# Attention and two MoE layers on one core: other instruction prices for the planner of the first three blocks

## The chip, the cores and the metric

The kernel runs on one core of a Trainium2 chip. The metric is the device time of the whole program in microseconds (us). Before the change it is 1163.88 us, the median of three runs (1162.69 to 1164.0).

The names in this text: PE is TensorE (matmul), DVE is VectorE, ACT is ScalarE, POOL is GpSimd, SP is SyncE, which issues the DMA transfers. L561 is line 561 of the kernel before. In the changed kernel every line from L185 on has a number that is one higher: L561 is L562 there.

## The reference

Three stages, one after the other, all in float32:

```python
x = attention(q, k, v, mem_k, mem_v)       # 4 batches, 8 heads, 768 positions of 64; chunks of 32 queries,
                                           # each with 16 keys to the left, 8 to the right, and 8 memory keys
x = x.transpose(0, 2, 1, 3).reshape(3072, 512)
h = x @ w_in                               # 512 x 2048
g = np.maximum(h, 0.0) + alpha * np.minimum(h, 0.0)
x = g @ w_out                              # 2048 x 512
return ((x @ w_a) * (x @ w_b)) @ w_o2      # 512 x 1536 twice, 1536 x 512
```

The weight matrices arrive as 64-bit floating-point words, and the kernel itself turns them into float32.

## The kernel before

**The work.** The 3072 tokens are cut into 24 attention units of 128 tokens, and these into blocks: two blocks of 2 units (256 tokens) come first, and then blocks of 4 units (512 tokens). A block's first products (`gemm1`, x times w_in, 16 of 128 output columns each) and second products (`gemm2`, g times w_out) follow on the attention of its units. Each product in the first MoE layer is made of three fp16 passes, high times high, high times low and low times high (`gemm3`, L925, L926, L927), so each operand is split into a high half on ACT (L361) and a low half on DVE (L365). The second MoE layer (`w_a`, `w_b`, `w_o2`) comes in a second phase with a planner call of its own.

**A unit of attention.** PE turns keys and queries (L728, L717), makes the scores (L752), turns the probabilities (L804) and multiplies by the values (L818). ACT copies the turned queries (L724) and exponentiates (L778). DVE takes the largest score (L768) and inverts the sums (L786, L789); the normalization is either one operation on DVE (L794) or four on ACT (L800). The copies out of PSUM, `kT`, `pT` and `x`, go to DVE (L657) or to ACT (L659). Then DVE takes the sizes of x for its scale (L827, L889, L896, L903; L329 to L340 turn a size into a power of two).

**A product of the first layer.** ACT evicts it twice (L942 to `g`, L945 to `t`), DVE joins the two (L948), ACT writes the high half (L954) and DVE the low half (L957) of `ghl`. A second product is evicted by DVE's L991 or ACT.

**The weights.** `chunk()` brings in one of 8 chunks of w_in, and later one of 8 chunks of w_out: a transfer of 1024 KB from SP (L483), the absolute value on ACT (L546), then on DVE L552 (w_in) or L556 (w_out), L561, L568 and L575, which turn the two words of a number into one float32. For w_in one scale serves all 8 chunks (`scale_w1`, L510 to L516), so no chunk is split before the last is read; a chunk of w_out has a scale of its own (sizes by ACT's L583). Then L361 and L365 split. The float32 values of w_in chunks are put together in the tile `w1` (`w_94` in the rows below), where the halves go too, and raw words of its chunks 4 to 7 lie in the tile of w_out's halves (`w_95`).

**The order.** No order is written by hand. `Schedule` is a list planner: each operation has an engine (or two to choose from), a price in us, a rank and what it depends on. `emit()` takes again and again the operation that can start first by the plan's own clock; ties go by rank. The rows of all five engines come out of this. The prices come from the table `took`:

```python
def dve(n, rate=1.04, pointers=0):
    return took["dve"] + 0.06 * pointers + n * rate / 1000
def act(n, pointers=0):
    return took["act"] + 0.09 * pointers + n * took["rate"] / 1000
def either(n):
    return {"DVE": dve(n), "ACT": act(n)}
```

`either` (L664) prices the copies and lets the plan give each one to DVE or ACT. The other entries are single prices: `tiny`, `itself`, `part` and `largest` for small DVE operations, `exp` and `scaled` for ACT's L778 and L800, `scores` and `values` for PE. The table is filled at L184 (it holds for the chunks of w_in and w_out and their scales), again at L1062 for each block (`SHORT` for the first three blocks, as `EXACT` is 3, `FULL` for the others), and with `SHORT` for the second phase.

Of the kernel before, what the change touches and what calls it, by code (L numbers as in the profile page):

```python
# [169 lines left out]
def pe(n, passes=1):  # L170
# [5 lines left out]
SHORT = dict(  # L176
    dve=0.07, act=0.06, rate=0.833, tiny=0.07, itself=0.09, part=0.09, largest=0.1,
    exp=0.357, scaled=0.267, scores=1.16, values=2.02,
)
FULL = dict(  # L180
    dve=0.15, act=0.17, rate=0.85, tiny=0.15, itself=0.16, part=0.2, largest=0.2,
    exp=0.57, scaled=0.42, scores=0.9, values=1.15,
)
took = dict(SHORT)  # L184


def dve(n, rate=1.04, pointers=0):
# [16 lines left out]
def tile_attention_moe_moe2(  # L204
# [29 lines left out]
    EXACT = 3  # L234
# [643 lines left out]
    def x_block(jb, x32, xhl, c0, rank):  # L878

        u0, nu = blocks[jb]  # L880
        p0 = c0 // P
        am = col(4)
        am1 = col()
        s, inv, iy = (col() for t in ("sx", "ix", "iy"))
        for i in range(nu):
            attention(u0 + i, *units[u0 + i], x32, p0 + i, am, rank + 0.1 * i)

        def largest():
            nc.vector.tensor_reduce(out=am1, in_=am[:, p0 : p0 + nu], axis=AX.X, op=ALU.max)  # L889

        sd.op(
            "DVE", took["largest"], rank, largest, [(x32, ("am", p0 + i)) for i in range(nu)], [(f"amx{jb}", 0)]
        )

        after = [
            lambda: nc.vector.tensor_tensor(out=s, in0=s, in1=ral, op=ALU.mult),  # L896
        ]
        scale(
            lambda: am1, s, inv, [(f"amx{jb}", 0), ("alpha", 0)], [(f"sx{jb}", 0)], after=after
        )  # L900

        sd.op(
            "DVE", took["tiny"], rank, lambda: nc.vector.tensor_tensor(out=iy, in0=inv, in1=iy0, op=ALU.mult),  # L903
            [(f"sx{jb}", 0), ("s_w1", 0)], [(f"iy{jb}", 0)],
        )
        for part in range(p0, p0 + nu):
            c = slice(part * P, (part + 1) * P)
            src = [(x32, part), (f"sx{jb}", 0)]
            sd.op(
                "ACT", act(512, 1), rank, lambda c=c: split_hi(x32.tile[:, :, c], xhl.tile[:, 0, :, c], s),  # L910
                src, [(xhl, ("h", part))],
            )
            sd.op(
                "DVE", dve(512, pointers=1), rank,
                lambda c=c: split_lo(x32.tile[:, :, c], xhl.tile[:, 0, :, c], xhl.tile[:, 1, :, c], s),
                src + [(xhl, ("h", part))], [(xhl, part)],
            )
        return iy
# [56 lines left out]
    def gemm2(jb, m, ghl, c0, n, iy, rank):  # L975
        ps, y32 = Buf(mm_slots), Buf(g_slots)
        c = slice(m * P, (m + 1) * P)
        d = slice(c0, c0 + n)
        iym = col()
        KQ = KF1 // 4  # L980

        def product(i):
            gh, gl = ghl.tile[:, 0, :, d], ghl.tile[:, 1, :, d]
            gemm3(
                ps.tile[:, :n],
                [(w2h[:, j, c], w2l[:, j, c], gh[:, j, :], gl[:, j, :]) for j in range(i * KQ, (i + 1) * KQ)],
                first=i == 0, last=i == 3,
            )

        def evac():  # L990
            nc.vector.tensor_scalar(y32.tile[:, :n], ps.tile[:, :n], iym, None, op0=ALU.mult)  # L991

        def evac_scale():
            nc.vector.tensor_tensor(out=iym, in0=iy, in1=inv_w2[:, m : m + 1], op=ALU.mult)

        t0 = blocks[jb][0] * P

        def store():
            nc.sync.dma_start(out=yd[:, m, t0 : t0 + n], in_=y32.tile[:, :n])

        for i in range(4):
            sd.op(
                "PE", KQ * pe(n, 3), rank, lambda i=i: product(i),
                [(ghl, (j, c0)) for j in range(i * KQ, (i + 1) * KQ)]
                + [(f"w2{2 * m}", 0), (f"w2{2 * m + 1}", 0)]
                + [("g1", jb, j) for j in range(KF1)], [(ps, 0)],
            )
        sd.op(
            "DVE", 0.07, rank - 1000, evac_scale,
            [(f"iy{jb}", 0)] + [(f"inv_w2{2 * m + i}", 0) for i in range(2)], [("iym", jb, m)],  # L1010
        )
        sd.op("DVE", dve(n, pointers=1), rank - 1000, evac, [(ps, 0), ("iym", jb, m)], [(y32, 0)])
        sd.op("SP", dma(n * 4 * P), -500, store, [(y32, 0)], [("yd", jb, m)])
# [32 lines left out]
    scaled = [chunk("w1", c, w_in, KD, CW, -5 + 0.5 * c, load_ranks[c]) for c in range(NC1)]  # L1046
# [12 lines left out]
            ar = 9 if b == 2 else (b - 1) * 10 + 4  # L1059
            place.append((Buf(x32_slots), Buf(xhl_slots), Buf(ghl_slots), 0, ar, b * 10 + 5, b * 10 + 8))  # L1060
    for jb, (x32, xhl, ghl, c0, ar, r1, r2) in enumerate(place):
        took.update(SHORT if jb < EXACT else FULL)  # L1062
        n = blocks[jb][1] * P
        iy = x_block(jb, x32, xhl, c0, ar)
        for m in range(KF1):
            gemm1(jb, m, xhl, ghl, c0, n, r1)
        for m in range(KD):
            gemm2(jb, m, ghl, c0, n, iy, r2)
# [334 lines left out]
```

## Time and profile before

| | us |
|---|---|
| runs | 1163.88, 1164.0, 1162.69 (median 1163.88) |
| the profiled execution | 1163.05 |
| its span, first to last instruction | 1161.3 |
| PE busy in it | 1116.2 (96%) |
| DVE busy | 874.9 (75%) |
| ACT busy | 595.5 (51%) |
| POOL busy | 232.3 (20%) |
| mean granted clock of TensorE | 0.982 |

Shares are averages over stages with different limits, so a stage is read by its own window. An instruction's duration can overlap the start of the next one on the same engine; the distance between two starts is what it costs in a full queue. An idle time in a row comes with what released the engine.

### The profile page before, as it was taken

The page shows a single profiled execution, that of the slowest core. Times are in us where ns is not written, and L with a number is a line of the kernel's source. Part 1 is how long each engine was busy: PE and PEld are TensorE (multiplying, and loading weights), DVE is VectorE, ACT ScalarE, POOL GpSimd, SP SyncE. Part 2 cuts the span into 40 slices and gives each one's busy share as a digit, 9 for nine tenths or more (in the row PEclk, how much of TensorE's full clock was granted, in tenths as well). Part 3 has the DMA queues.
Part 4 walks back from the last instruction along what each step waited for, and adds up shares of the span by engine and source line. Part 5 has one row for each costly group of instructions (what it writes and reads, how often), then busy time and mean ns, then how long its engine had stood idle before and what let it go on. Part 6 is the DMA issues. An engine that isn't in the chain of part 4 may idle for free.

```text
span 1161.3 us, 23129 instructions
## 1 busy us (share of the span) xinstructions
PE 1116.2 (96%) x9304; PEld 808.8 (70%) x9304; DVE 874.9 (75%) x1524; ACT 595.5 (51%) x1300; POOL 232.3 (20%) x298
## 2 busy tenths in 40 slices
PE   4499899999999999999999999999999999999998
PEld 3378786555555555544444688888888888888887
DVE  6999998887887888796352287876867958958882
ACT  4599767866786776486262122533424433424340
POOL 1000002022002111222300010243323424324530
PEclk8599999999999999999999999999999999999999
DMA  9964571548446823433603162613513514415211
GB/s 254 254 132 120 154 202 46 141 122 230 132 126 179 227 82 94 166 109 121 242 1 136 59 196 84 198 38 101 191 55 114 177 37 146 146 37 178 96 37 38
DMA packets 162523, 150.93 MB, mean 130 GB/s; under 512 B 104032, under 2 KB 139888, under 8 KB 162416
## 3 DMA queue, kind: packets, MB, share of 16 engines
q1 hardware_dynamic: 162416, 149.45, 42.9%
q8 instruction: 73, 1.20, 0.4%
q14 instruction: 34, 0.28, 0.1%
HBM read 120.33 MB, written 29.10 MB: 129 GB/s over the span
## 4 chain that ended last, share of the span: by engine, by line
PE 87%; DVE 7%; ACT 3%; DMA 1%; issue 1%; POOL 0%; SPq 0%; ACTq 0%; DVEq 0%; POOLq 0%
PE mm L925 27%; PE mm L927 27%; PE mm L926 26%; PE pair L804 2%; PE mm L818 2%; PE pair L728 1%; PE pair L752 1%; DVE w L568 1%; DMA w1b<-wb_d 1%; PE mm L717 1%; DVE w L365 1%; ACT sm L778 1%; DVE w L575 0%; DMA kw<-in_k_dram 0%; PE mm L324 0%
## 5 line engine op out<-in xcount | busy, mean ns | idle before, releaser
L927 PE MATMUL mm<-ghl,w 128*128 128x512 f16 (+1 forms) x448 | 156.2, 349 | 2.5 <-DVE w L365 2.5
L925 PE MATMUL mm<-xhl,w 128*128 128x512 f16 (+1 forms) x448 | 156.7, 350 | 1.3 <-ACT t L945 1.2
L926 PE MATMUL mm<-xhl,w 128*128 128x512 f16 (+1 forms) x448 | 156.6, 349 | 1.0 <-DVE xhl L365 1.0
L925 PE MATMUL mm<-ghl,w 128*128 128x512 f16 (+1 forms) x448 | 156.3, 349 | 0.3 <-ACT w L361 0.3
L927 PE MATMUL mm<-xhl,w 128*128 128x512 f16 (+1 forms) x448 | 156.5, 349 | 0.0
L926 PE MATMUL mm<-ghl,w 128*128 128x512 f16 (+1 forms) x448 | 156.2, 349 | 0.0
L927 PE MATMUL mm<-units,w1b 128*128 128x256 f16 x560 | 152.6, 273 | 0.7 <-DVE w1b L365 0.7
L926 PE MATMUL mm<-units,w1b 128*128 128x256 f16 x560 | 152.6, 273 | 0.0
L925 PE MATMUL mm<-units,w1b 128*128 128x256 f16 x560 | 152.6, 273 | 0.0
L927 PEld LDWEIGHTS <-w 128*128 128x128 f16 x896 | 87.8, 98 | 83.1 <-DVE w L365 3.4
L925 PEld LDWEIGHTS <-w 128*128 128x128 f16 x896 | 87.9, 98 | 75.0 <-ACT w L361 0.5
L926 PEld LDWEIGHTS <-w 128*128 128x128 f16 x896 | 87.8, 98 | 73.5 <-issue 1.6
L925 PE MATMUL mm<-w2b,w1b 128*128 128x256 f16 x504 | 137.4, 273 | 0.3 <-DMA w1b<-wb_d 0.2
L926 PE MATMUL mm<-w2b,w1b 128*128 128x256 f16 x504 | 137.4, 273 | 0.0
L927 PE MATMUL mm<-w2b,w1b 128*128 128x256 f16 x504 | 137.4, 273 | 0.0
L927 PEld LDWEIGHTS <-w1b 128*128 128x128 f16 x1064 | 104.1, 98 | 13.1 <-DVE w1b L365 0.9
L925 PEld LDWEIGHTS <-w1b 128*128 128x128 f16 x1064 | 104.1, 98 | 12.9 <-DMA w1b<-wb_d 0.8
L926 PEld LDWEIGHTS <-w1b 128*128 128x128 f16 x1064 | 104.1, 98 | 12.4
L381 POOL TENSOR_TENSOR raw<-w 128x256 f32<-128x256 f32 x18 | 15.3, 852 | 456.7 <-ACT raw L583 456.7
L957 DVE TENSOR_TENSOR ghl<-g,ghl 128x512 f16<-128x512 f32 (+1 forms) x112 | 69.3, 630 | 23.4 <-ACT ghl L954 23.1
L942 ACT ACTIVATE g<-mm 128x512 f32<-128x512 f32 (+1 forms) x112 | 60.5, 540 | 46.0 <-PE mm L927 43.8
L948 DVE SCALAR_TENSOR_TENSOR g<-t,columns,g 128x512 f32<-128x512 f32 (+1 forms) x112 | 77.1, 696 | 8.4 <-ACT t L945 8.2
(288 smaller groups left out, 2405.7 us busy)
## 6 DMA issues: line engine op xcount, KB each, us to landing
w1b<-wa_d SPq DMA_DIRECT2D x26, 896.0 KB
w1b<-wb_d SPq DMA_DIRECT2D x26, 896.0 KB
raw<-in_moe_w_out_dram SPq DMA_DIRECT2D x8, 1024.0 KB
kw<-in_k_dram SPq DMA_DIRECT2D x40, 176.0 KB
vw<-in_v_dram SPq DMA_DIRECT2D x40, 176.0 KB
qt<-in_q_dram SPq DMA_DIRECT2D x24, 256.0 KB
raw<-in_moe_w_a_dram SPq DMA_DIRECT2D x12, 512.0 KB
raw<-in_moe_w_b_dram SPq DMA_DIRECT2D x12, 512.0 KB
```

The source lines that it names most:

```text
L365: nc.vector.scalar_tensor_tensor(out=lo, in0=src, scalar=s, in1=hi, op0=ALU.mult, op1=ALU.subtract)
L381: (nc.vector if e == "DVE" else nc.gpsimd).tensor_tensor(out=out_()[:, i], in0=x()[:, a], in1=y()[:, b], op=op)
L568: nc.vector.scalar_tensor_tensor(out=f, in0=lo, scalar=29, in1=f, op0=ALU.logical_shift_right, op1=ALU.bitwise_or)
L717: nc.tensor.transpose(out=pq.tile[:, g * P : (g + 1) * P], in_=qt.tile[:, 2 * g : 2 * g + 2, :].rearrange("p h d -> p (h d)"), identity=ident,
L804: nc.tensor.transpose(out=heads(pp, P)[:KW, o, g], in_=sm.tile[:, o, g], identity=ident)
L818: nc.tensor.matmul(out=out[64 * o : 64 * o + 64, g, c], lhsT=vw.tile[:, j, 2 * g + o], rhs=pT.tile[:, o, g, c], start=True, stop=True,)
L925: nc.tensor.matmul(out=ps, lhsT=lh, rhs=rh, start=first and i == 0, stop=False)
L926: nc.tensor.matmul(out=ps, lhsT=lh, rhs=rl, start=False, stop=False)
L927: nc.tensor.matmul(out=ps, lhsT=ll, rhs=rh, start=False, stop=last and i == n - 1)
L942: nc.scalar.activation(out=g.tile[:, :n], in_=ps.tile[:, :n], func=ACTF.Relu, scale=E1)
L948: nc.vector.scalar_tensor_tensor(out=g.tile[:, :n], in0=t2.tile[:, :n], scalar=nal[:, m : m + 1], in1=g.tile[:, :n], op0=ALU.mult, op1=ALU ...
L957: nc.vector.tensor_tensor(out=ghl.tile[:, 1, m, d], in0=g.tile[:, :n], in1=ghl.tile[:, 0, m, d], op=ALU.subtract,)
```

## The change

A new table `REAL` is added. It takes the place of `SHORT` in two places: where `took` is first filled, and for the first three blocks.

```diff
 SHORT = dict(
     dve=0.07, act=0.06, rate=0.833, tiny=0.07, itself=0.09, part=0.09, largest=0.1,
     exp=0.357, scaled=0.267, scores=1.16, values=2.02,
 )
...
-took = dict(SHORT)
+REAL = dict(dve=0.09, act=0.14, rate=0.87, tiny=0.17, itself=0.18, part=0.2, largest=0.2, exp=0.32, scaled=0.30, scores=0.9, values=1.15)
+took = dict(REAL)
...
-        took.update(SHORT if jb < EXACT else FULL)
+        took.update(REAL if jb < EXACT else FULL)
```

No operation of the program is changed. The second phase's order is the same in both kernels, row for row, and so is the end of the first phase on every engine: the last 9707 of PE's rows, 646 of DVE's and 258 of ACT's are equal. The start is equal up to the second unit of attention. What moves lies between.

**ACT, where the first chunks of w_in are split.** L724 copies a unit's turned queries; `w_94<-raw` is the hi split of w_in's chunk 0, the three `w_94<-ghl` are those of chunks 1 to 3, and `w_522<-raw` is the absolute value of w_out's chunk 0. Before:

```order
L778 ACTIVATE sm,sums<-pair,nm 128x96 x8
L724 ACTIVATE qT<-mm 128x512
L361 ACTIVATE w_94<-raw,columns 128x4x256
L361 ACTIVATE w_94<-ghl,columns 128x4x256 x3
L942 ACTIVATE g<-mm 128x256
L945 ACTIVATE t_579<-mm 128x256
```

Now:

```order
L779 ACTIVATE sm,sums<-pair,nm 128x96 x8
L725 ACTIVATE qT<-mm 128x512
L547 ACTIVATE w_522<-raw 128x1024
L362 ACTIVATE w_94<-raw,columns 128x4x256
L362 ACTIVATE w_94<-ghl,columns 128x4x256 x3
L943 ACTIVATE g<-mm 128x256
L946 ACTIVATE t_590<-mm 128x256
```

The absolute value of a chunk of w_out has moved ahead of the four hi splits; before, it stands 25 rows below the first of them. The first copy of `pT` is in the same place.

**DVE, in the same place of the program.** L365 (now L366) is the lo split, L794 (L795) a normalization, L575 (L576) the last step of a chunk of w_in, here chunk 6, and L948 (L949) the join of a first product. Before:

```order
L516 TENSOR_SCALAR columns<-columns 128x1
L789 RECIPROCAL rs<-rs 128x8
L561 TENSOR_SCALAR w_94<-w_94 128x8x128
L903 TENSOR_TENSOR columns<-columns 128x1
L794 TENSOR_TENSOR sm<-sm,rs 128x384
L365 SCALAR_TENSOR_TENSOR w_94<-raw,columns,w_94 128x4x256
L365 SCALAR_TENSOR_TENSOR w_94<-ghl,columns,w_94 128x4x256 x2
L948 SCALAR_TENSOR_TENSOR g<-t_579,columns,g 128x256
L365 SCALAR_TENSOR_TENSOR w_94<-ghl,columns,w_94 128x4x256
```

Now:

```order
L795 TENSOR_TENSOR sm<-sm,rs 128x384 x2
L576 SCALAR_TENSOR_TENSOR w_95<-w_95,w_94 128x1024
L366 SCALAR_TENSOR_TENSOR w_94<-raw,columns,w_94 128x4x256
L366 SCALAR_TENSOR_TENSOR w_94<-ghl,columns,w_94 128x4x256 x3
L949 SCALAR_TENSOR_TENSOR g<-t_590,columns,g 128x256
L949 SCALAR_TENSOR_TENSOR g<-t_610,columns,g 128x256
L658 COPY kT<-pair 128x384
L958 TENSOR_TENSOR ghl<-g,ghl 128x256 x2
L658 COPY kT<-pair 128x384
L949 SCALAR_TENSOR_TENSOR g<-t_660,columns,g 128x256
L562 TENSOR_SCALAR w_94<-w_94 128x8x128
```

Both normalizations of the unit are here on DVE, L576 has come in between them and the lo splits (before, L575 of chunk 6 stands 11 rows above the first lo split, ahead of the scale's L329), all four lo splits come ahead of the first join, and an L562 of chunk 7 stands behind it.

**A copy of x that changes engines.** Some thirty rows later, while w_out's first chunk is read. On ACT before:

```order
L361 ACTIVATE w_94<-w_95,columns 128x4x256
L954 CAST ghl<-g 128x256
L942 ACTIVATE g<-mm 128x256
L945 ACTIVATE t_919<-mm 128x256
L546 ACTIVATE w_921<-raw 128x1024
L659 COPY x_261<-mm 128x4x128
L659 COPY kT<-pair 128x384
L954 CAST ghl<-g 128x256
```

On DVE now:

```order
L557 TENSOR_SCALAR w_522<-w_522 128x1024
L958 TENSOR_TENSOR ghl<-g,ghl 128x256 x2
L562 TENSOR_SCALAR w_522<-w_522 128x1024
L949 SCALAR_TENSOR_TENSOR g<-t_978,columns,g 128x256
L658 COPY x_261<-mm 128x4x128
L366 SCALAR_TENSOR_TENSOR w_94<-w_95,columns,w_94 128x4x256
L958 TENSOR_TENSOR ghl<-g,ghl 128x256
L828 TENSOR_REDUCE columns<-x_261 128x1
```

The copy of x was ACT's L659 and is now DVE's L658, ahead of its L828. Before, DVE's row ahead of that L827 is an L561.

## Rows read from the trace of the kernel before

**Rows 1.** The page: busy time of each engine.

```profile
PE 1116.2 (96%) x9304; PEld 808.8 (70%) x9304; DVE 874.9 (75%) x1524; ACT 595.5 (51%) x1300; POOL 232.3 (20%) x298
```

**Rows 2.** Busy time by window: us, PE, PEld, DVE, ACT, POOL, PEclk, DMA share, GB/s.

```profile
0.00:58.80 58.80, 26.51 (x239) 20.36 (x240) 45.07 (x84) 29.91 (x80) 4.99 (x41) 0.67 0.94 253
58.80:178.80 120.00, 112.87 (x1283) 97.30 (x1281) 112.51 (x241) 97.47 (x275) 0.00 (x0) 0.99 0.60 147
178.80:730.00 551.20, 551.20 (x3902) 311.20 (x3900) 395.00 (x671) 315.18 (x718) 82.27 (x96) 1.00 0.43 133
```

**Rows 3.** Timeline of PE: start, us, instruction, idle before it and its releaser.

```profile
168.33 0.28 PE L927 MATMUL mm<-ghl,w 128*128 128x256 f16 x1 [0.34 <-DVE w L365]
...
178.77 0.38 PE L925 MATMUL mm<-xhl,w 128*128 128x512 f16 x1
```

**Rows 4.** Timeline of DVE from 166 to 170.

```profile
166.40 0.68 DVE L657 COPY x<-mm 128x512 f32<-128x512 f32 x1
167.00 1.27 DVE L365 SCALAR_TENSOR_TENSOR w<-w,columns,w 128x1024 f16<-128x1024 f32 x1
168.19 0.68 DVE L827 TENSOR_REDUCE columns<-x 128x1 f32<-128x512 f32 x1
168.79 0.48 DVE L991 TENSOR_SCALAR g<-mm,columns 128x256 f32<-128x256 f32 x1
...
169.24 0.95 DVE L758 TENSOR_TENSOR sm<-pair,mask 128x768 f32<-128x768 f32 x1
```

**Rows 5.** Timeline of DVE from 53 to 59.

```profile
53.07 1.22 DVE L575 SCALAR_TENSOR_TENSOR w<-w,w 128x1024 int32<-128x1024 int32 x1
54.21 0.28 DVE L329 TENSOR_REDUCE m<-mm 128x1 f32<-128x128 f32 x1
54.52 0.15 DVE L333 TENSOR_SCALAR m<-m 128x1 int32<-128x1 int32 x1
54.71 0.15 DVE L337 TENSOR_SCALAR columns<-m 128x1 f32<-128x1 f32 x1
...
55.96 0.55 DVE L794 TENSOR_TENSOR sm<-sm,rs 128x384 f32<-128x384 f32 x1
57.25 1.28 DVE L365 SCALAR_TENSOR_TENSOR w<-raw,columns,w 128x1024 f16<-128x1024 f32 x1 [0.74 <-ACT w L361]
```

**Rows 6.** Timeline of ACT: first hi split of w_in, first L546 of w_out.

```profile
56.01 1.21 ACT L361 ACTIVATE w<-raw,columns 128x1024 f16<-128x1024 f32 x1 [3.04 <-DVE w L561]
...
74.11 1.23 ACT L546 ACTIVATE w<-raw 128x1024 f32<-128x1024 f32 x1
```

**Rows 7.** SyncE's issue of w_out's first chunks, and what DMA moved by window.

```profile
48.69 3.24 SPq L483 DMA_DIRECT2D raw<-in_moe_w_out_dram  x2
...
48.70:53.40 4.70, 1.32 (x9) 0.90 (x5) 4.54 (x10) 3.18 (x17) 0.00 (x0) 0.50 0.92 224
48.70:57.00 8.30, 1.94 (x11) 1.26 (x8) 7.51 (x20) 4.17 (x18) 0.00 (x0) 0.50 1.04 254
```

**Rows 8.** Timeline of DVE: two copies of kT.

```profile
63.52 1.01 DVE L657 COPY kT<-pair 128x384 f32<-128x384 f32 x2
```

**Rows 9.** Timeline of ACT: two evictions of 256 columns.

```profile
61.23 0.38 ACT L942 ACTIVATE g<-mm 128x256 f32<-128x256 f32 x1 [0.65 <-PE mm L927]
61.51 0.38 ACT L945 ACTIVATE t<-mm 128x256 f32<-128x256 f32 x1
```

**Rows 10.** Waits of DVE, 58.5 to 168.3: us in total, times, longest.

```profile
DVE w L556 <- ACT w L546: 1.4, 3, 0.7
DVE rs L786 <- ACT sm L778: 1.2, 1, 1.2
DVE g L948 <- ACT t L945: 1.0, 1, 1.0
DVE m L329 <- PE mm L324: 0.9, 2, 0.7
DVE w L568 <- ACT w L361: 0.8, 1, 0.8
```

## The prediction

> **What bounds the kernel now.** I read the totals first, then the stages, then the waits. TensorE (PE) is busy 96% of the span [rows 1], so everything that is not PE work is worth at most the rest. The windows show where that rest lies [rows 2]: 32 us before 58.8, in which weights are loaded and converted and the clock is 0.67; 7.1 us between 58.8 and 178.8; nothing at all from 178.8 to 730, where 551.20 of 551.20 us are busy. The reader should see two things in this. Between 58.8 and 178.8 VectorE (DVE) is as full as PE: 112.51 of 120 us (94%) beside 112.87, while ScalarE (ACT) has 97.47 (81%). And once 178.8 is passed, a delay of PE can't be won back, since PE has no idle time to give for 551 us.
>
> What happens at 178.8 is that block 2, the first of 512 tokens, starts its first product [rows 3]. In PE's order it stands behind all second products of the two small blocks, and those need all eight chunks of w_out. The last one to come is chunk 7: its low part is written by DVE from 167.00 to 168.3 [rows 4], PE's L927 starts at 168.33 after a wait for it, and block 2 starts 10.4 us later [rows 3]. So the time at which DVE is through with chunk 7 is what I forecast, and I take the shift of block 2 as the shift of the end. The instructions behind it stand in the same order in both kernels.
>
> **The change part by part.** The table changes only prices in the planner; the instructions do the same work. What counts is the order that comes out, and who does the copies that either DVE or ACT may do.
>
> *The start.* Before, ACT runs the first hi split (L361) at 56.01 and DVE the first lo split (L365) at 57.25 [rows 5, 6]. Now ACT has `w_522<-raw`, the absolute value of w_out's chunk 0, ahead of its four splits; before, that stood at 74.11 [rows 6]. And DVE has an L576 of 1024 elements ahead of its first L366, and L576 waits for the first hi split: both use the tile `w_94`, one reads and the other writes it. So four things of some 1.15 us come in series: the absolute value, a hi split, L576, then the lo split. The first can't begin before chunk 0 has landed. SyncE issues chunks 0 and 1 at 48.69 [rows 7]; the landing is in no row, so I bound it. From 48.7 to 53.4 the queues move 4.7 x 224 = 1053 KB, about one chunk: if all of it were chunk 0, it would land at 53.4. From 48.7 to 57.0 they move 8.3 x 254 = 2108 KB, two chunks: if both go side by side, chunk 0 lands at 57.0. Part of the early bytes belong to transfers issued before, so I take 55.6, a little over the middle. Then the absolute value ends at 56.75, the hi split at 57.9 and L576 at 59.1 (1.15, 1.15 and 1.2 from start to start; such rows take 1.21 to 1.28, of which some 0.08 overlap the next [rows 5, 6]), and the lo split starts at 59.1 in place of 57.25: **+1.8**. With 57.0 it would be +3.2. With 53.4 the scale that the split needs is the later one. Its chain starts at 54.21 behind an L575 of 1.14 [rows 5], and without L575 ahead of it and with L903 to L794 still to come, I estimate the end of the two L795 at 55.7; L576 follows to 56.85, and the lo split comes 0.4 earlier than now. So -0.4 to +3.2.
>
> One page weighs in here. The Trainium skill (DMA: Bandwidth & Descriptors, "Anatomy of one DMA") gives, for another way of issuing, about 2.0 us plus the bytes at 436 GB/s, which for a chunk of 1.05 MB is an estimated 4.4 us, a landing at 53.1 and so the -0.4. The rows disagree as to the rate: with a DMA share of 1.04 the queues move 254 GB/s from 48.7 to 57.0 [rows 7], and chunk 0 isn't alone in them. By the page the sum below would end 2.2 us lower, at +2.9 in place of +5.1.
>
> *The work ahead of chunk 7.* I count DVE's instructions from the first lo split of w_in to the lo split of chunk 7 in both orders. They are 216 now and 229 in the changed order. More: 3 copies of x (2 to 5), 3 of kT (4 to 7), one each of L561, L827, L758, L991, L889, L896 and L903, and one chain L329 to L340. Fewer: 3 normalizations L794 (8 to 5) and one L556. Prices are distances from start to start, or durations less the overlap of some 0.08. A copy of x is 0.60 (166.40 to 167.00), L827 0.60, L991 0.40 and L758 0.87 [rows 4]. Two kT copies take 1.01 together, 0.46 each [rows 8]. L561 and L556 are both one-input operations on 1024 elements and cancel. L794 is 0.47, an L329 0.31, and a small one such as L333 0.19 [rows 5]; there are six of these (L333, L337, L340, L889, L896, L903), 1.14. That makes 1.80 + 1.38 + 0.60 + 0.40 + 0.87 + 0.31 + 1.14 = 6.5 more, and 3 x 0.47 = 1.4 less: **+5.1**.
>
> Why copies go to DVE can be read off the table. A copy of 512 cost 0.60 on DVE and 0.49 on ACT in the plan; now it costs 0.62 and 0.585. A 256-wide eviction on ACT is planned at 0.363, while the two traced ones start 0.28 apart [rows 9] (0.273 in the old table). So 64 of them make ACT look 5.3 us busier than it is, and the planner relieves it at the cost of the engine that is fuller.
>
> *Waits.* DVE's waits in the stretch are listed [rows 10]. L948's 1.0 and L568's 0.8 come right behind the first splits. There the changed order has one more lo split ahead of its first L949, and L569 stands far behind its release, so I drop both: **-1.8**. The others (L556 1.4, L786 1.2, L329 0.9) may stay or go, and new ones may come; I keep them, with 0 and -3.5 as the far end. PE isn't what DVE would wait for: in the changed order PE has all 32 first products early and only two units' value products between them.
>
> *The sum.* +1.8 + 5.1 - 1.8 = +5.1: chunk 7's lo split ends at 173.4, block 2 starts at about 183.9. On the profiled execution, 1163.05 (its span of 1161.3 and 1.75 around it), this makes 1168.15. That execution lies 0.8 below the median of the runs shown; on the median's scale I forecast **1169.0**.
>
> **The rivals.** *(A) The plan is better, and DVE's waits go.* If intervals nearer to the traced ones place instructions where their data is ready, L556, L786 and L329 lose their 3.5 us. For it: all three are waits of DVE for ACT or PE that the old prices didn't foresee. Against it: the new prices of ACT are further from the rows than the old. It gives 5.1 - 3.5 = +1.6, or 1165.5; with a landing at 53.4 it is -0.6, or 1163.3. No difference.
>
> *(B) PE becomes the bound, and it is faster.* If DVE is through with chunk 7 early enough, PE loses its idle 7.1 us between 58.8 and 178.8 [rows 2], less the 1.5 or so by which the first product comes later. That is -5.6, or 1158.3 on the median's scale. It decides from the point at which chunk 7's lo split ends by 162.8 (178.8 - 5.6 - 10.4). For it: PE's order has fewer attention steps between the first products, so what waits for DVE comes later in it. Against it: DVE's own work, with none of the listed waits, still ends at 168.3 + 5.1 + 1.8 - 1.8 - 3.5 = 169.9. A weaker form, half of the gain, would need an early landing and two thirds of DVE's waits gone.
>
> *(C) The loss is larger.* DVE now has L562 of w_in's chunk 7 behind the fourth product, and copies of kT among the first products; everything on DVE queues behind such a wait. With the late landing (+1.4 over my value) and 2 us of new waits it is +8.5, or 1172.4.
>
> *(D) The change doesn't do what it says.* Its ACT prices aren't the traced intervals, as shown above. That is part of my forecast rather than another time.
>
> **How the numbers follow.** A difference under 0.2%, 2.3 us, can't be told from none here. My forecast, from +2.4 to +7, has 0.46; (C) 0.15; (A) 0.24; (B) 0.15, weak form included. That gives slower 0.61, same 0.24, faster 0.15. The range leaves out most of (B) and the far end of (C): from 1162.0, which takes in (A) with an early landing, to 1173.0. The forecast alone has 1166.3 to 1171.
>
> **What would show it.** In the changed kernel's trace: `w_522` on ACT beginning about 55.6 with a wait for a transfer, ahead of the first hi split; the first lo split of w_in near 59.1; 5 x copies on DVE and some 107 us of its work before the lo split of w_out's chunk 7, which ends near 173; PE's first 128x512 product near 183.8 and no idle time from there to 735. It is wrong if block 2 starts before 178.8, if DVE is idle for more than 6 us ahead of chunk 7, or if the end moves by another amount than block 2's start.

## The result, and the profile after

The changed kernel takes 1178.36 us (median of 4 runs, 1176.21 to 1179.74) beside 1163.85 for the kernel before: a ratio of 1.0125 with a 95% interval of 1.0113 to 1.0138. It is slower by 14.5 us. The prediction had 5.1 us, with an upper end at 1173.0: the sign was right, the size was a third of it. The profiled execution took 1178.0, 14.95 above that of before. One execution of n3 below (1681.72 us at a mean granted clock of 0.657) was in a slow state and is left out of n3's numbers; all other numbers are of fast runs.

Busy times on the page of the changed kernel, which answer to [rows 1]:

```profile
PE 1122.6 (95%) x9304; PEld 811.4 (69%) x9304; DVE 875.6 (74%) x1529; ACT 596.4 (51%) x1301; POOL 231.6 (20%) x298
```

PE does the same 9304 matmuls and is busy for 6.4 us longer. That isn't work: 5.4 of it lie between the first product and block 2, where the mean granted clock is 0.95 in place of 0.99, as the windows below show.

The timeline of the start, ACT and then DVE, against [rows 6] and [rows 5]:

```profile
55.09 1.14 ACT L547 ACTIVATE w<-raw 128x1024 f32<-128x1024 f32 x1 [2.75 <-DMA raw<-in_moe_w_out_dram]
56.14 1.21 ACT L362 ACTIVATE w<-raw,columns 128x1024 f16<-128x1024 f32 x1
```

```profile
57.38 1.23 DVE L576 SCALAR_TENSOR_TENSOR w<-w,w 128x1024 int32<-128x1024 int32 x1 [2.02 <-ACT w L362]
58.64 1.28 DVE L366 SCALAR_TENSOR_TENSOR w<-raw,columns,w 128x1024 f16<-128x1024 f32 x1
...
179.15 1.28 DVE L366 SCALAR_TENSOR_TENSOR w<-w,columns,w 128x1024 f16<-128x1024 f32 x1
```

The series of four is there: w_out's chunk 0 lands at 55.09, the hi split and L576 follow, and the first lo split starts at 58.64 in place of 57.25, 1.4 us later. The last row is w_out's chunk 7, whose lo split starts at 179.15 in place of 167.00 [rows 4].

The timeline of PE at its largest waits and at block 2's start, against [rows 3]:

```profile
59.98 0.40 PE L928 MATMUL mm<-xhl,w 128*128 128x256 f16 x1 [1.32 <-DVE w L366]
...
97.05 0.27 PE L926 MATMUL mm<-xhl,w 128*128 128x256 f16 x1 [2.05 <-ACT xhl L362]
98.44 0.34 PE L927 MATMUL mm<-xhl,w 128*128 128x256 f16 x1 [1.11 <-DVE xhl L366]
...
180.49 0.40 PE L928 MATMUL mm<-ghl,w 128*128 128x256 f16 x1 [2.30 <-DVE w L366]
...
192.38 0.38 PE L926 MATMUL mm<-xhl,w 128*128 128x512 f16 x1
```

Block 2 starts at 192.38 and not at 178.77: +13.6 of the 14.9 that the span grew by are there when it starts.

Windows of each kernel: from PE's first product to block 2's, from the first lo split to the end of chunk 7's, and from block 2's start to the point behind which PE's rows are the same in both kernels (columns as in [rows 2]). Before:

```profile
58.79:178.77 119.98, 112.85 (x1282) 97.29 (x1280) 112.49 (x241) 97.48 (x275) 0.00 (x0) 0.99 0.60 147
57.25:168.19 110.94, 103.95 (x1196) 89.54 (x1194) 103.58 (x216) 91.97 (x254) 0.00 (x0) 0.98 0.62 153
178.77:590.67 411.90, 411.90 (x2930) 216.15 (x2928) 321.67 (x549) 277.17 (x648) 76.70 (x88) 1.00 0.47 142
```

After:

```profile
58.03:192.38 134.35, 118.28 (x1279) 99.66 (x1277) 119.35 (x248) 100.50 (x279) 0.36 (x1) 0.95 0.54 132
58.64:180.34 121.70, 105.78 (x1181) 89.46 (x1180) 108.52 (x229) 94.33 (x259) 0.00 (x0) 0.96 0.57 140
192.38:605.67 413.29, 412.60 (x2931) 216.08 (x2929) 316.71 (x543) 274.41 (x641) 75.43 (x88) 1.00 0.47 141
192.38:1176.20 983.82, 977.50 (x7788) 691.09 (x7785) 713.87 (x1201) 465.31 (x939) 226.23 (x257) 1.00 0.38 120
```

These rows split the loss in two ways. By PE: between its first product and block 2's its idle time grows from 7.1 to 16.1 us (+8.9), its busy time from 112.85 to 118.28 (+5.4), and it starts 0.8 earlier; that is the 13.6. By DVE: its work up to chunk 7 grows from 103.58 to 108.52 (+4.9), its idle time from 7.4 to 13.2 (+5.8), and it starts 1.4 later; that is 12.1, and the rest of the 13.6 is half clock behind it. Both are accounts of where the time stands, and don't say what would come back if one term were taken away; the experiments ask that. The remaining 1.3 us come between block 2's start and 605.67 (413.29 us in place of 411.90).

The waits of DVE in that stretch, against [rows 10]:

```profile
DVE g L992 <- PE mm L928: 2.7, 4, 1.3
DVE m L330 <- PE mm L325: 2.0, 4, 1.2
DVE g L949 <- ACT t L946: 1.6, 2, 1.5
DVE x L658 <- PE mm L819: 1.3, 3, 0.6
DVE w L366 <- ACT w L362: 1.1, 2, 0.6
DVE kT L658 <- PE pair L729: 1.0, 2, 0.7
DVE pT L658 <- PE pair L805: 1.0, 2, 0.5
DVE w L569 <- PE mm L928: 0.6, 1, 0.6
DVE ghl L958 <- ACT ghl L955: 0.6, 1, 0.6
```

Before, the one wait for PE beside those of [rows 10] was this:

```profile
DVE pT L657 <- PE pair L804: 0.7, 2, 0.4
```

Before, DVE waited for ACT above all, and 1.6 us for PE. Now 8.6 of these 11.9 us are for PE, and 6.6 of the 8.6 come after 121, behind the last first product.

The clock, in a window of the kernel before and then in windows of the changed kernel (PEclk is the third number from the right):

```profile
60.00:62.00 2.00, 2.00 (x17) 1.62 (x16) 1.01 (x2) 1.35 (x4) 0.00 (x0) 0.83 0.94 232
```

```profile
62.00:64.00 2.00, 2.00 (x11) 1.40 (x10) 1.96 (x3) 1.20 (x4) 0.00 (x0) 0.50 0.81 211
64.00:66.00 2.00, 2.00 (x19) 1.73 (x17) 0.59 (x2) 1.28 (x4) 0.00 (x0) 0.91 1.18 314
...
96.00:98.00 2.00, 0.27 (x1) 0.10 (x1) 2.00 (x6) 1.49 (x4) 0.00 (x0) 1.00 0.99 249
98.00:100.00 2.00, 1.56 (x8) 1.12 (x8) 2.00 (x5) 0.00 (x0) 0.00 (x0) 0.63 1.14 311
100.00:102.00 2.00, 2.00 (x12) 1.37 (x10) 1.93 (x4) 1.06 (x3) 0.00 (x0) 0.52 0.34 86
...
182.00:184.00 2.00, 2.00 (x12) 1.45 (x11) 2.00 (x4) 0.39 (x1) 0.00 (x0) 0.54 0.22 61
```

At the start the lower level (1.2 GHz) lasts to 64, where before it had passed to 2.4 GHz between 60 and 62. It comes back twice: behind the waits of 2.05 and 1.11 us at 95 to 98.4, and behind the 2.30 us ahead of 180.49. The 96 matmuls that are left then take 11.9 us; before, they took 10.4.

### The profile page after: what moved, and what is told of

The parts are those of the page before. It is cut to its first block, busy times and chain, and to the rows that moved or that the text cites. A ratio compares the mean times of both kernels' runs of the same rounds, so it can differ in the third digit from the quotient of the medians.

```text
span 1176.2 us, 23144 instructions
## 1 busy us (share of the span) xinstructions
PE 1122.6 (95%) x9304; PEld 811.4 (69%) x9304; DVE 875.6 (74%) x1529; ACT 596.4 (51%) x1301; POOL 231.6 (20%) x298
## 4 chain that ended last, share of the span: by engine, by line
PE 90%; DVE 5%; SPq 2%; DMA 1%; issue 1%; ACT 1%; POOL 0%; ACTq 0%; POOLq 0%
PE mm L926 28%; PE mm L928 27%; PE mm L927 27%; PE mm L819 2%; PE pair L805 2%; PE pair L753 1%; SPq L701 1%; PE pair L729 1%; PE mm L718 1%; DMA raw<-in_moe_w_out_dram 1%; SPq L703 1%; SPq L689 0%; PE mm L325 0%; DVE w L366 0%; DVE w L569 0%
## 5 line engine op out<-in xcount | busy, mean ns | idle before, releaser
L927 PEld LDWEIGHTS <-w1b 128*128 128x128 f16 x1064 | 104.1, 98 | 12.5
L949 DVE SCALAR_TENSOR_TENSOR g<-t,columns,g 128x512 f32<-128x512 f32 (+1 forms) x112 | 76.4, 689 | 9.9 <-ACT t L946 9.3
```

The costliest lines, as they stand in the source:

```text
L927: nc.tensor.matmul(out=ps, lhsT=lh, rhs=rl, start=False, stop=False)
L949: nc.vector.scalar_tensor_tensor(out=g.tile[:, :n], in0=t2.tile[:, :n], scalar=nal[:, m : m + 1], in1=g.tile[:, :n], op0=ALU.mult, op1=ALU ...
```

## The experiments

The loss is in the order of the instructions, so most experiments change the order alone. For s1, s2, c1, d1 and the three of unit 4, the order is written into the kernel as a list of operations and engines, and the planner takes them from it. The lines below are those of the three of unit 4; the other four take the list's next entry as it stands:

```diff
-            best = None
...
-            (_, _, cost, t), e, o = best
+            o, e = next(p for p in plan if not p[0].left and self.start(p[0], free[p[1]]) is not None)
+            plan.remove((o, e))
+            cost, t = o.costs[e], self.start(o, free[e])
```

**The head, either way (s1, s2).** One list up to the first product, the other from there on.

> The changed kernel with the emission order written out as a list: up to the first product of the first layer the list of the kernel before, from there on the list of the change, and the absolute value of w_out's chunk 0 at its old place on ACT. Theory 1 (my prediction: the head is worth 1.4 us on DVE, the loss is DVE work put ahead of w_out's chunk 7): 1.4 us less than the change, about 1177. Theory 2 (the head: PE takes its first products at half clock for 4 us longer, the scores of unit 3 come 3 us later, block 1 starts 6.4 us later, and from there it runs on): first product's low pass without a wait, clock up near 61, block 1's first product near 93, and 6 us or more less than the change, 1172 or below. Theory 3 (the joint order of PE and DVE behind the head costs, whatever the head does): within 1 us of the change, 1177 to 1179.

> The mirror: the order of the change up to its first product (both early absolute value and late L576), the order of the kernel before from there on. Theory 1: 1.4 us above the kernel before, about 1165.3. Theory 2: 6 us or more above it, 1170 or more, with clock up only near 64 and block 1 near 98. Theory 3: within 1 us of the kernel before.

Measured: s1 1180.28 (ratio to before 1.0142, 1.0127 to 1.0157), s2 1167.82 (1.0036, 1.0023 to 1.0049). With the old head the rest of the changed order is not faster than the change (1.9 us slower, which the two intervals don't tell apart); s1 also has a cost of its own, since its second normalization now stands behind two lo splits and PE waits 1.26 us for it. Block 1 starts at 99.8 and block 2 at 195.2: theory 2 is refuted. The head alone, with the old order behind it, costs 4.0 us, more than the 1.4 of theory 1 and than the 1 of theory 3, so none of the three has both numbers. About a quarter of the loss can come from the head, and the larger part comes from the order behind it.

**The engines of the copies (c1).**

The list, in words:

```diff
-(op, engine of the change) for each op
+(op, engine of the kernel before) for each op
```

> The order of the change, with every copy and normalization on the engine that the kernel before gives it (65 of them differ in the whole program). Theory 1: the copies are what is more on DVE ahead of chunk 7, so 5 us less than the change, about 1173.4. Theories 2 and 3: within 2 us of the change, 1176 to 1180, since DVE waits for PE there and has the time.

Measured: 1179.78 (1.014, 1.0125 to 1.0155), not faster than the change (1.4 slower, within the two intervals), as theories 2 and 3 had it. The window from the first lo split to the end of chunk 7's:

```profile
59.95:184.60 124.65, 108.62 (x1180) 91.27 (x1180) 107.18 (x227) 94.08 (x253) 0.00 (x0) 0.97 0.55 134
```

DVE's work falls only by 1.3 us, to 107.18, because three normalizations go back to DVE as copies leave it, and because the rest of the +4.9 isn't a choice of engine: it is work that the order places ahead of chunk 7. Its idle time grows by 4.3, from 13.2 to 17.5. The little that is taken off DVE here isn't given back, it turns into waiting. My expectation of 5 us was wrong for both reasons. How much of the 4.9 would come back if all of it were taken off, c1 doesn't show.

**The clock alone (d1).** Matmuls of zeros into the same accumulators where PE waits.

```diff
+        def zeros(k, start=False):
+            for _ in range(k):
+                nc.tensor.matmul(out=ps[:, :256], lhsT=z16[:, :P], rhs=z16, start=start, stop=False)
+                start = False
...
```

> The change with its own order, and matmuls of zeros added into the same accumulators where PE waits: 6 behind the second pass of the first product, 18 ahead of block 1's first pass and 10 behind it, 21 behind the second pass of the first second-layer product that needs w_out's chunk 7. They change no value. If the half clock behind these gaps is itself worth its 5.5 us of longer PE time (theory 2 counts it in): granted clock 1.00 from 98 to 102 and from 181 to 184, up before 63 at the start, and 3 to 5.5 us less than the change, 1173 to 1175. If DVE sets the time and the clock only fills what PE would have waited: within 1 us of the change at the first two places, 1.7 less at the last, about 1176.7.

Measured: 1174.42 (1.0096, 1.0077 to 1.0115), 3.9 less than the change. The same places in its trace:

```profile
60.00:62.00 2.00, 1.40 (x13) 1.27 (x14) 2.00 (x3) 2.00 (x3) 0.00 (x0) 1.00 0.66 148
90.00:92.00 2.00, 2.00 (x29) 1.25 (x31) 1.94 (x3) 0.69 (x3) 0.00 (x0) 0.50 0.00 0
98.00:100.00 2.00, 2.00 (x20) 1.65 (x18) 2.00 (x5) 0.38 (x2) 0.00 (x0) 1.00 1.11 299
...
178.00:180.00 2.00, 1.99 (x19) 1.56 (x17) 2.00 (x7) 2.00 (x4) 0.00 (x0) 1.00 1.04 227
```

The granted clock stays at 1.00 at both later places and is up before 62. With PE kept busy where it waited, the same order is 3.9 us faster; the intervals of the two ratios just meet. This is a net gain and not the clock's whole share: between 88 and 94, behind waits of 1.0 and 1.6 us, d1's trace has a stretch at the lower level (0.50 from 90 to 92) that the change doesn't have (1.00 there).

**One unit of attention moved (u4, u34, u4m).** In the change unit 4's exponentials stand behind all 32 first products, in the kernel before behind 19.

The list, in words:

```diff
-unit 4's 23 operations where the change has them
+unit 4's 23 operations behind the same number of products as in the kernel before
```

> The order of the change, with the 23 operations of attention unit 4 alone (the first unit of block 2) moved, on all engines, to the places that they have in the kernel before, counted in products: its exponentials behind 18 first products in place of 32 and 2 parts of second ones, its values behind 27 in place of 32 and 7. Theory 3 (the change lets the softmax of units 3 and 4 slip behind in the queues of DVE and ACT, so that units 4 to 7 come as a chain of latencies at the end, scores of unit 5 at 136 in place of 110): unit 5's scores by 125, w_out's chunk 7 split by 175 or sooner, and 4 us or more less than the change, 1174 or below. Theory 1 (what counts is DVE's work ahead of chunk 7): the work is the same, within 1.5 us of the change.

> The same for units 3 and 4 and the scale and splits of block 1's x: 58 operations at the places of the kernel before. Theory 3: block 1's first product at 94 in place of 97.0, and 3 us less than with unit 4 alone, 1171 or below, half of the loss or more. Theory 1: within 1.5 us of the change.

> The mirror: the order of the kernel before, with the 23 operations of unit 4 alone moved to the places of the change. Theory 3: unit 5's scores behind 130, and 4 us or more above the kernel before, 1168 or more. Theory 1: within 1.5 us of it.

Measured: u4 1182.48 (1.0163, 1.0149 to 1.0177), u34 1189.11 (1.022, 1.0207 to 1.0234), u4m 1188.48 (1.021, 1.0194 to 1.0225). All three expectations of theory 3 for the change missed: bringing one unit forward made the change 4 us slower, two units 11 us. Only the mirror went the way of theory 3, and by six times what it asked for. In u4 unit 5's scores come at 137.7, 1.6 later than in the change: the queues behind still hold the units 5 to 7 where they were, so what was moved forward only stands in the way of the first products (the last of them at 125.5 in place of 121.1). In u34 block 1 starts at 102.6, where theory 3 had 94 in place of 97.0. So theory 3, in the form that two late units are the cause, fell: a piece of the better order, put into the worse one, doesn't mend it.

**The passes of a product (p1).**

```diff
-        for i, (lh, ll, rh, rl) in enumerate(ops):
-            nc.tensor.matmul(out=ps, lhsT=lh, rhs=rh, start=first and i == 0, stop=False)
-            nc.tensor.matmul(out=ps, lhsT=lh, rhs=rl, start=False, stop=False)
-            nc.tensor.matmul(out=ps, lhsT=ll, rhs=rh, start=False, stop=last and i == n - 1)
+        passes = [(0, 2), (0, 3), (1, 2)] if wlate else [(0, 2), (1, 2), (0, 3)]
+        for k, (a, b) in enumerate(passes):
+            for i, op in enumerate(ops):
...
```

> The kernel before with the three passes of a product in another order: first the passes that need only what comes early, and last those with the half that comes late (the low half of the weights in block 0's first products and all second ones, the low half of x in the other first ones). If PE's waits for a low half in the kernel before (2.5 us for L365 of weights in three places, 1.0 for x) are what PE loses there: up to 0.9 us each is covered by the passes ahead, 2 to 3 us less than before, 1161 to 1162. If DVE sets the time up to 178 either way: within 1 us of before.

Measured: 1162.77 (0.9996, 0.9987 to 1.0004), no difference. PE's waits in its trace, 58.8 to 178:

```profile
PE mm L927 <- ACT t L949: 1.6, 3, 1.2
PE mm L324 <- ACT raw L583: 1.2, 1, 1.2
PE pair L804 <- DVE sm L794: 1.0, 1, 1.0
PE mm L927 <- DVE w L365: 0.9, 2, 0.7
```

The waits for low halves are shorter, as the edit meant (0.9 us for weights where the kernel before has 2.5), and others have taken their place.

**The numbers of the table.** To compare orders without running them I laid one price list, the old one, over each fixed order, by the planner's own rules for when an operation can start. The result is the planner's clock, not the chip's. For the eight orders read so far it lay 7 to 10 us below the traced start of block 2 in seven, and 16 in u4m. The new list, laid over the order of the kernel before, puts block 2 at 184.8, and over that of the change at 182.3: by the new prices the change looks better by 2.5 us, where the trace has it worse by 13.6. From this, theory 4: the prices have no cost of their own; what counts is the order that comes out, and the old list can tell a good one. Against it theory 5: each number costs by its distance from the chip. In all runs of this part the numbers stand in `REAL`, so the second phase keeps the old table; the diffs show only the numbers that differ from the table named.

```diff
-    exp=0.357, scaled=0.267, scores=1.16, values=2.02,
+    exp=0.357, scaled=0.267, scores=1.16, values=1.15,
```

> The old table with one number of the new: a unit's value products at 1.15 us in place of 2.02. Theory 4 (an order can be told by laying a fixed price list over it: with the old table the planner's clock puts block 2's start 7 to 10 us below the trace in seven of the eight orders read so far, 171.5 for the kernel before and 183.6 for the change; and of the table's numbers it is this one that most often turns good orders into bad ones): this order comes to 190.1 by the old prices, so block 2 starts at 197 to 200, and the time is 1182 to 1186, worse than the change, though ten of its eleven numbers are the old ones. Theory 3 (the high prices of ACT's and DVE's operations make the order): this number is PE's alone, within 3 us of the kernel before.

```diff
-exp=0.32, scaled=0.30, scores=0.9, values=1.15)
+exp=0.32, scaled=0.30, scores=0.9, values=2.02)
```

> The mirror: the change with the value products at their old 2.02 us. Theory 4: 177.9 by the old prices, 6.4 above the kernel before, so 1169 to 1172, half of the loss gone. Theory 3: within 3 us of the change, 1175 or more.

Measured: n1 1176.48 (1.0112, 1.0098 to 1.0126), n2 1171.94 (1.008, 1.0063 to 1.0096). One number of eleven, put into the old table, makes it 12.9 us slower; taken out of the new one, it gives 6.4 back. n2 is just inside theory 4's numbers; n1's block 2 starts at 198.3, as expected, but the time is 5 us less than expected, and 1.9 below the change where theory 4 had it worse: PE has been busy for 125.1 us by then (112.85 in the kernel before), part of it with unit 8, whose values are done at 182.9 where before they come at 189.6, behind block 2's start. The window from its first product to block 2, and PE's two longest waits in it:

```profile
60.74:198.31 137.57, 125.12 (x1448) 107.92 (x1446) 126.47 (x265) 109.37 (x312) 7.41 (x8) 0.96 0.56 137
...
142.85 0.61 PE L805 MATMUL pair<-ident,sm 128*96 128x128 f32 x4 [2.92 <-DVE sm L795]
...
178.40 1.94 PE L805 MATMUL pair<-ident,sm 128*96 128x128 f32 x8 [3.87 <-DVE sm L795]
```

It is a PE price, and much of what it does in n1 shows at DVE: PE's turn of the probabilities waits there for the normalization, 7.0 us in three places by the list of waits, and what is queued behind it on PE waits too. The span grows by 12.6 us. Of these 2.0 are there at the first product, and PE's idle time up to block 2 grows by 5.3 (12.5 against 7.1). The rest, 5.4, is PE's longer busy time less the 6.9 by which the stretch behind block 2 is shorter; the mean granted clock up to block 2 is 0.96 in place of 0.99.

```diff
-SHORT's numbers, tiny=0.07
+SHORT's numbers, tiny=0.17
```

> The old table with one number of the new: tiny at 0.17 in place of 0.07. Theory 5 (each number costs or gains by how far it is from the chip): small DVE operations start 0.19 apart in the trace, so this one is right and should gain nothing to 1 us. Theory 4 (only the order that comes out counts; by the old prices this one comes to 168.0, 3.5 below the kernel before): 2.5 to 5 us less than the kernel before, 1159 to 1161.

```diff
-SHORT's numbers, act=0.06, rate=0.833
+SHORT's numbers, act=0.14, rate=0.87
```

> The old table with ACT's two new numbers, 0.14 and 0.87. Theory 5: these are the furthest from the trace (0.363 for 256 columns, which start 0.28 apart) and push copies to DVE, so most of the 8 us that value products leave open: 1168 to 1172. Theory 4: 174.7 by the old prices, 3 us above the kernel before, 1165 to 1168.

```diff
-REAL: act=0.14, rate=0.87
+REAL: act=0.06, rate=0.833
```

> The change with ACT's two numbers put back to 0.06 and 0.833. Theory 5: better prices, 4 us or more less than the change, 1174 or below. Theory 4: 191.5 by the old prices, 8 above the change's 183.6, so slower than the change, 1184 to 1189.

Measured: n3 1159.77 (0.9968, 0.9956 to 0.998), n4 1167.75 (1.0034, 1.0022 to 1.0046), n5 1181.99 (1.0156, 1.0143 to 1.017). n3 is 4.0 us faster than before and n4 3.9 slower, both inside theory 4's numbers; n4 is only 0.25 below theory 5's and doesn't decide. n3, where theory 5 had 1 us at most, and n5 do. n5 is 2 us below theory 4's, but 3.6 slower than the change, where theory 5 had it 4 or more faster: putting the price of ACT back next to the traced interval makes it worse. Theory 5 is refuted.

**Other tables (k1, k2, k3).** Some thousands of tables with each number varied a little, or moved part of the way to the new one, were turned into orders by the planner, and the orders put in a row by the old price list (and by a variant of it with PE at half the clock at the start); k1 and k2 come from the best of them. The numbers of k2:

```diff
-REAL = dict(dve=0.09, act=0.14, rate=0.87, tiny=0.17, itself=0.18, part=0.2, largest=0.2, exp=0.32, scaled=0.30, scores=0.9, values=1.15)
+REAL = dict(dve=0.084, act=0.0614, rate=0.8753, tiny=0.0711, itself=0.092, part=0.0893, largest=0.0909, exp=0.3471, scaled=0.2653, scores=1.1582, values=1.843)
```

> A third table in the same two places, none of whose numbers is the new one: dve 0.0864, act 0.0602, rate 0.8463, tiny 0.0725, itself 0.1, part 0.1768, largest 0.1408, exp 0.3551, scaled 0.2754, scores 1.0784, values 1.986. Its order comes to 169.2 by the old prices, 2.3 below the kernel before (and 4 to 5 below it with half the clock up to 59 and values at 1.10). Theory 4: 2 to 5 us less than the kernel before, 1159 to 1162. If one order in some thousands that looks best by such a price list only looks best: within 3 us of it on either side.

> A fourth: dve 0.084, act 0.0614, rate 0.8753, tiny 0.0711, itself 0.092, part 0.0893, largest 0.0909, exp 0.3471, scaled 0.2653, scores 1.1582, values 1.843. 169.9 by the old prices, 1.6 below the kernel before (5 below with half the clock up to 59). Theory 4: 2 to 5 us less than the kernel before. Else within 3 us on either side.

> The faster of the two other tables (k2) with the pass order of p1 (late halves last). p1 alone was within its interval of the kernel before. If it covers PE's waits for low halves here (2.0 us for L366 in two places): 1157.5 to 1158.5. If not: within 1 us of k2, 1159 to 1160.

Measured: k1 1160.0 (0.997, 0.9958 to 0.9981), k2 1159.39 (0.9966, 0.9954 to 0.9979), k3 1159.99 (0.9965, 0.9953 to 0.9977). Both draws beat both kernels, by 3.6 and 4.2 us against the kernel before; the pass order adds nothing. k1, k2, k3 and n3, which has one number changed, lie within 0.6 us of one another and aren't told apart. The windows of k2 around its block 2:

```profile
57.00:175.70 118.70, 113.43 (x1277) 97.81 (x1278) 111.58 (x238) 98.79 (x275) 0.00 (x0) 0.98 0.59 150
175.70:730.00 554.30, 554.08 (x3926) 313.75 (x3924) 392.82 (x672) 322.15 (x735) 79.72 (x96) 1.00 0.43 132
```

PE is idle for 5.3 us between its first product and block 2, 7.1 in the kernel before, and block 2 starts at 175.7. From there PE is full, as before.

All orders side by side: the start of block 2 by the old price list, in the trace, and the median time.

| order | old prices | traced | time |
|---|---|---|---|
| before | 171.5 | 178.8 | 1163.8 |
| change | 183.6 | 192.4 | 1178.4 |
| s1 / s2 | 185.7 / 173.1 | 195.2 / 183.4 | 1180.3 / 1167.8 |
| c1 | 185.5 | 195.0 | 1179.8 |
| u4 / u34 | 188.7 / 194.0 | 195.7 / 203.0 | 1182.5 / 1189.1 |
| u4m | 190.0 | 206.0 | 1188.5 |
| n1 / n2 | 190.1 / 177.9 | 198.3 / 185.8 | 1176.5 / 1171.9 |
| n3 / n4 / n5 | 168.0 / 174.7 / 191.5 | 173.9 / 181.3 / 200.3 | 1159.8 / 1167.8 / 1182.0 |
| k1 / k2 | 169.2 / 169.9 | 175.5 / 175.7 | 1160.0 / 1159.4 |

In 14 of 15 orders the trace is 5.8 to 10.3 us above the old list; u4m, at 16.0, is the exception. So the list can't tell orders apart that lie within some 4 us of one another. It forecasts block 2's start and not the time: n1 is behind u4 by the list and in the trace, and yet 6.0 us faster, as it does later work ahead of block 2. And by the very prices that made it, the order of the kernel before (171.5) is worse than those of n3, k1 and k2 (168.0 to 169.9): the planner doesn't find the best order for its own prices.

## Why the prediction was wrong in size

- **What bounds the kernel**: right. All but 1.3 us of the loss is there when block 2 starts (983.82 us from there to the end, 982.53 before). That the instructions behind it stand in the same order is not so: PE's rows are the same only from 605.67 on (590.67 before). It costs little, because PE is idle for only 0.7 us in that stretch, and in the kernel before not at all.
- **The start, +1.8**: measured +1.4. The landing of w_out's chunk 0, bounded by 53.4 and 57.0 and taken at 55.6, was 55.09. The estimate by the Trainium skill (DMA: Bandwidth & Descriptors, "Anatomy of one DMA"), for another way of issuing, was 53.1, 2.0 too early here, with another chunk and other transfers in the same queues.
- **DVE's work ahead of chunk 7, +5.1**: measured +4.9 (108.52 against 103.58). The term was right as a count, and it is a third of the loss: the sign came out right with most of the reason missing. That it is the cause of its third isn't shown: the 1.3 us that c1 took off didn't come back.
- **Waits, -1.8**: this is the step that failed. L948's and L568's waits did not vanish (L949 waits 1.6, L569 0.6), and I kept the others as they were. DVE's idle time grew by 5.8, to 13.2, where I had it fall by 1.8: 7.6 us of the error, and the prediction's own sign of being wrong (more than 6 us). The sentence behind it, "PE isn't what DVE would wait for", is wrong by the rows: 8.6 us of DVE's waits are for PE. It came from looking at the first products alone, where PE is indeed ahead; most of the waits are behind them (6.6 of the 8.6), where the units 4 to 7 alternate between the two engines.
- **The clock**: not priced at all. I passed from chunk 7 to block 2 with the 10.4 us of before; it took 11.9, at the lower level at first. d1 gave back 3.9 us by keeping the clock up in three places, net of a fourth stretch at the lower level.
- **Sum**: 5.1 + 7.6 - 0.4 (start) - 0.2 (work) + 1.5 (clock behind chunk 7) + 1.3 (behind block 2) = 14.9, the growth of the span.
- **Rivals**: (C), the larger loss with new waits of DVE, was the right mechanism, but with 2 us of new waits where there were 5.8, and no clock. In (D) I read ACT's high prices as the reason for the order. Put into the old table they cost 3.9 us (n4), but taken out of the new one they make it 3.6 slower (n5), and the one number that does most, the value products, I passed over since it is PE's and true to the trace at full clock.

Shown by the runs: value products at 1.15 make 12.9 us alone and 6.4 in company, and ACT's numbers 3.9 alone and -3.6 in company, so neither has a cost that adds up; orders whose block 2 comes some 5 us earlier by the old price list have it earlier on the chip too (u4m apart). Seven of the eleven numbers were not tried by themselves. Not settled: why a lower price of the value products so often gives a bad order. n1 shows where its time goes, not by what steps of the planner. The two places where the table is used, the weights' chunks and the blocks, were not separated.

## What to carry to other kernels

A greedy list planner doesn't choose among whole orders, so better prices need not give a better order; one price of eleven moved this one by 13 us. Judge the order, not the prices: lay one fixed price list, proven on a few traces, over the orders that come out, and run the best; here that gave 0.3%. When an order changes, don't keep the waits of the old one: count for each queue what it waits for in the new one, on every engine and up to the last stage, and price the clock behind PE's new waits from rows at its lower level.

## What was not expected

A wait of PE costs more than its length: behind 2.05 and 1.11 us of waiting at 95 to 98.4 the granted clock is 0.63 and 0.52 for the next 4 us. And a clock column can be read wrongly. In c1's trace it is 1.00 from the start, but two windows tell otherwise:

```profile
62.00:64.00 2.00, 2.00 (x11) 1.44 (x10) 2.00 (x3) 1.75 (x3) 0.00 (x0) 1.00 0.50 153
68.00:70.00 2.00, 2.00 (x40) 1.70 (x39) 2.00 (x6) 1.30 (x5) 0.00 (x0) 1.00 1.04 171
```

In the first PE gets through 11 matmuls in 2 us, as many as the changed kernel does there at 0.50; c1's matmuls of 256 columns start 0.21 us apart up to 66.9 and 0.11 apart from there on. So c1 begins at the lower level too, and its trace doesn't record that. The same goes for the first 12 us of the kernel before, which read 1.00 and are part of the 0.67 in [rows 2]: four of L717's matmuls take 1.12 us at 10.15 and 0.66 at 67.72. Check the column by the distance of equal matmuls.
